# ScalarE scales the upper words of doubles, and two more head pairs use split exponents

## The chip, the cores and the metric

One core of a Trainium2 chip runs the whole program. The time is in device microseconds (us). Of the kernel before there are three runs: 1375.54, 1376.45 and 1377.31 us, so the median is 1376.45 us. TensorE (PE) multiplies matrices, VectorE (DVE), ScalarE (ACT) and GpSimd (POOL) do element work, SyncE (SP) issues the DMA transfers. Each engine takes its instructions strictly in the order in which the program gives them.

## The reference

```python
def _attn_ref(q, k, v, g_q, g_k):            # batch 8, heads 12, seq 448, head_dim 64, float32
    q_n, k_n = rmsnorm(q, g_q), rmsnorm(k, g_k)
    scores = q_n @ k_n.T / sqrt(64)
    attn = exp(scores - max(scores)); attn = attn / (sum(attn) + 1e-9)
    return attn @ v

def _moe_ref(x, w_in, w_out, s, b):          # x: 3584 x 768, w_in: 768 x 2048, w_out: 2048 x 768
    r = maximum(x @ w_in, 0)
    return (s * r * r + b) @ w_out
```

The two weight matrices come as float64. [...]

## The kernel before

**Pairs and steps.** The 96 heads are worked in 48 pairs, p = 0 to 47. A pair takes eight steps of the main loop (L784), four chunks of 128 keys for each of its two heads, so pair p has the steps 8p to 8p+7. In a step s the program issues, in this order: the two matmuls of the transposed scores of chunk s (`score_t`, L496 and L499), two matmuls of the feed-forward layer (`filler`), the exponent of chunk s on ACT (`exponent`), the transfers of finished feed-forward rows (`keep_r`, L228), the jobs listed for this step (`jobs[s]`), a score matmul for a later pair (`score`, L453 or L451), two more of the feed-forward layer, the ReLU copies on ACT (`rectify`, L218), the maximum of those scores on DVE (L464), the jobs of the kind `late`, the product of the exponents of chunk s-2 with v (`weigh`, L557), and two more feed-forward matmuls. The feed-forward matmuls start with step 57; they are the work that fills TensorE from there on. After the last pair comes the second layer alone.

**Exponents.** For pairs below `NV = PLAIN` (11) the exponents are float32 in SBUF (tile `e`, L511) and meet v in one float32 matmul, which is two records in the trace. For the later pairs the exponent stays in PSUM (L515), ACT copies it to a rounded high part `ah` (L523), DVE writes the rest to `low` (L538; the fourth chunk's rest goes into the unused half of `ah`), and three matmuls of the fast type (two for the fourth chunk) meet v. For that v too is split, into `vs`, by ACT (L353) and POOL (L354), three steps before the pair begins (`split_v`).

**Rooms.** A tile with a tag and one buffer is a room: a new tile of the tag waits until the last reader of the old one is done, wherever in the program that reader stands. The room `vr` has one buffer and two kinds of tenants. For an even pair below `TURNED` (12) it takes the second half of that pair's rows, loaded by `load_rows` (L241 to L245) 28 steps before that half's first step and last read by `turn`, the four transposes of L277, 14 steps before it. For pair 10 these are the steps 56 and 70. From pair `NV` on it takes v (`load_v`, L343 and L344), loaded nine steps before the pair begins; for pairs below `NV` v goes to two other tiles, five steps before (L338 to L341). The room `low` has the `low` parts of all split pairs and, before them, the pieces of w_in named in `THIRD`; the other pieces share two buffers of the tag `w64`.

**Doubles.** w_in comes in 24 pieces, loaded by `load_piece` and converted at the steps of `PACE`, in the steps 8 to 93; w_out in 24 groups, converted from step 112 on (`PACE_OUT`). `to_single` issues on DVE a shift of the upper word (L149), two combinations of words (L152, L154) and a comparison with multiplication (L157), which makes numbers below a bound zero by the square that ACT took (L150). Each `yield` ends what one call of `next` issues; `convert` and `convert_out` (both `late`) make the calls, five steps for a piece.

The part of the loop's lists that carries v, before and after the change alike:

```python
            at(s0 - (9 if p >= NV else 5), load_v, p)
            if p >= NV:
                at(s0 - 3, split_v, p)
```

Of the kernel before, what the change touches and what calls it, by code (L numbers as in the profile page):

```python
# [9 lines left out]
F32 = mybir.dt.float32  # L10
F32R = mybir.dt.float32r
I32 = mybir.dt.int32
AF = mybir.ActivationFunctionType
ALU = mybir.AluOpType
# [4 lines left out]

ORDERED = {ENGINE.PE, ENGINE.Activation, ENGINE.DVE, ENGINE.Pool, ENGINE.SP}  # L20

LEAST = (1 + 1 / 8) * 2.0 ** (0x70 - 127)

START = 9

# [23 lines left out]

APART = 8  # L50

PLAIN = 11

THIRD = (11, 14, 17)

PACE_OUT = tuple(48 * b + 16 + 8 * i for b in range(2, 8) for i in range(4))

GAP = 2


@with_exitstack
def attention_then_relu2_ffn(
# [30 lines left out]
    V, S, G, T = nc.vector, nc.scalar, nc.gpsimd, nc.tensor  # L93

    NPAIR, P, _, SEQ = kq.shape
# [7 lines left out]
    TILES = 2 * SEQ // P  # L103
    NV = PLAIN
    NQ = 4
# [9 lines left out]
    WI = 512  # L115
# [27 lines left out]
        bank = free.pop(0)  # L143
        return ps.tile([P, 512], F32, tag=bank, name=name), bank

    def to_single(w, a, m):

        low, high = w[:, :, 0], w[:, :, 1]
        V.tensor_scalar(a, high, 3, 0x3FFFFFF8, ALU.logical_shift_left, ALU.bitwise_and)  # L149
        S.activation(m, high.bitcast(F32), AF.Square)  # L150
        yield
        V.scalar_tensor_tensor(a, high, -0x40000000, a, ALU.bitwise_and, ALU.bitwise_or)  # L152
        yield
        V.scalar_tensor_tensor(a, low, 29, a, ALU.logical_shift_right, ALU.bitwise_or)  # L154
        yield
        af = a.bitcast(F32)
        V.scalar_tensor_tensor(af, m.bitcast(F32), LEAST * LEAST, af, ALU.is_ge, ALU.mult)  # L157

    def load_double(room, dst_hi, dst_lo, src):

        w, words, m = room
        nc.sync.dma_start(w.rearrange("p n t -> p (n t)"), src)
        yield
        a = words()
        yield from to_single(w, a, m)
        for _ in range(GAP):
            yield
        S.copy(dst_hi, a.bitcast(F32))
        yield
        G.tensor_tensor(dst_lo, a.bitcast(F32), dst_hi.bitcast(F32), ALU.subtract)  # L170
        yield
# [5 lines left out]
    def parts_of_w_in():  # L177

        for i in range(NS):
            whi[i] = wpool.tile([P, NCC, FS], F32R, tag=f"wh{i}", name=f"wih{i}")  # L180
            wlo[i] = wpool.tile([P, NCC, FS], F32R, tag=f"wl{i}", name=f"wil{i}")
            for c0 in range(0, FS, WI):
                for cc in range(NCC):
                    f0 = 2 * (i * FS + c0)
                    src = w_in32[cc * P : (cc + 1) * P, f0 : f0 + 2 * WI]
                    yield whi[i][:, cc, c0 : c0 + WI], wlo[i][:, cc, c0 : c0 + WI], src
# [43 lines left out]
    with tc.tile_pool(name="apool", bufs=1) as ap:  # L230
# [395 lines left out]
        def pieces():  # L626
            for i, (hi, lo, src) in enumerate(parts_of_w_in()):
                if i in THIRD:
                    w = ap.tile([P, WI, 2], I32, tag="low", name=f"w64i{i}")
                else:  # L630
                    w = ap.tile([P, WI, 2], I32, tag="w64", bufs=2, name=f"w64i{i}")

                def words(i=i):
                    return ap.tile([P, WI], I32, tag="wa", bufs=3, name=f"wai{i}")

                yield load_double((w, words, hi), hi, lo, src)

        todo = pieces()
        loaded = []

        def load_piece():

            g = next(todo, None)
            if g is not None:
                next(g)
                loaded.append(g)

        def convert(i, n):

            for _ in range((2, 1, 1, 2, 1)[n]):  # L650
                next(loaded[i], None)

        wides, singles = {}, {}

        def load_out(i):
# [3 lines left out]
            for h in range(2):  # L659
                r0 = (h * NH + f) * P  # L660
                src = w_out32[r0 : r0 + P].rearrange("p (e n) -> p e n", e=2)
                nc.sync.dma_start(to[:, h], src[:, :, 2 * c * P : 2 * (c + 1) * P])

        def convert_out(i, n):

            if n == 0:
                a, m = (
                    ap.tile([P, WI], I32, tag="wa", bufs=3, name=f"wao{i}_{k}") for k in range(2)
                )
                singles[i] = to_single(wides.pop(i), a, m.bitcast(F32)), a, m  # L670
            steps, a, m = singles[i]
            if n < 4:
                next(steps, None)
                return
            w = a.bitcast(F32).rearrange("p (h e n) -> p h e n", h=2, e=2)
            t = m.bitcast(F32).rearrange("p (k n) -> p k n", k=4)
            V.tensor_tensor(t[:, 0:2], w[:, :, 1], w[:, 0], ALU.subtract)
            V.tensor_tensor(t[:, 2], w[:, 1, 1], t[:, 0], ALU.subtract)
            V.tensor_tensor(t[:, 3], w[:, 1, 0], t[:, 2], ALU.subtract)

        def keep_out(i):
            f, c = divmod(i, NQ3)
            _, a, m = singles.pop(i)
            for d, of in ((b_d, a), (t_d, m)):
                nc.sync.dma_start(
                    d[:, :, f, c * P : (c + 1) * P].rearrange("k p n -> p k n"),
                    of.bitcast(F32).rearrange("p (k n) -> p k n", k=4),
                )

        late = (scale_q, split_last, convert, invert, convert_out, split_lows)  # L690

        fill = iter(())
# [9 lines left out]
        def at(s_, f, *a):  # L702
            jobs[s_].append((f, a))

        for i, s_ in enumerate(PACE):
            if i != THIRD[-1]:
                at(s_ + 3, load_piece)
        for p in range(NPAIR):
# [7 lines left out]
            for j in range(2):  # L716
                s1 = s0 + 4 * j
                steps = SOONER.get((p, j), (s1 - 20, s1 - 14, s1 - 13, s1 - 10, s1 - 6))
# [34 lines left out]
        for b in range(B):  # L753
            for g in range(NCC):
                s_ = W * NP * (b + 1) + START + (-3, -2, 0, 1, 2, 3)[g]
                if b == 0:
                    s_ = W * g + 24 if g < NCC - 1 else s_
# [3 lines left out]
        for s_ in (1, 7, 53):  # L761
            at(s_, load_piece)
        for i, s_ in enumerate(PACE):
            for n in range(5):
                at(STEPS[i][n] if i in STEPS else s_ + n, convert, i, n)
        for i, s_ in enumerate(PACE_OUT):
            at(s_ - 4, load_out, i)
            for n in range(5):
                at(s_ + n, convert_out, i, n)
            at(s_ + 6, keep_out, i)  # L770
# [11 lines left out]
        with tc.manual_schedule(engines=ORDERED):  # L782
            begun = []
            for s_ in range(FIRST, NSLOT + START + NCC):  # L784
# [34 lines left out]
                b, m = divmod(s_ + 1 - START, W * NP)  # L819
# [7 lines left out]
    with tc.tile_pool(name="opool", bufs=1) as op:  # L827

        def half(pool, tag, shape, name):
            return pool.tile(shape, F32R, tag=tag, name=name)  # L830
# [5 lines left out]
        room = [half(op, f"c2{x}", [P, 3, NH, P], f"room{x}") for x in "hl"]  # L836
# [144 lines left out]
        with tc.manual_schedule(engines=ORDERED):  # L981
# [29 lines left out]
            for n in range(7 * NG):  # L1011
                g, k = divmod(n, 7)
# [78 lines left out]
```

## Time and profile before

| | |
|---|---|
| runs | 1375.54, 1376.45, 1377.31 us |
| span of the profiled execution | 1375.6 us (0.85 us under the median) |
| PE busy | 99% of the span |
| DVE, ACT, POOL busy | 77%, 68%, 44% |
| granted TensorE clock | 1.00 in every stretch |
| steps 0 to 57 | about 15.8 to 112.8 us |
| steps 58 to 71 | about 112.8 to 152.7 us |
| steps 72 to 87 (pairs 9 and 10) | 152.74 to 194.83 us |
| rest of the pairs, then the second layer | to 893 us, then to the end |

A matmul's end is modelled in the profile, so the distance between the starts of two matmuls says what one costs, not its listed length. On DVE a listed length can hold time in which the instruction has started and can't go on.

### The profile page before, as it was taken

What the parts mean: (1) busy time and instruction counts of PE and PEld (TensorE: products, weight loads), DVE (VectorE), ACT (ScalarE), POOL (GpSimd) and SP (SyncE); (2) the same over time, 40 slices, a digit from 0 to 9 for tenths busy, and PEclk for the clock granted to TensorE, in tenths of its full rate; (3) what the DMA queues carried; (4) which work ended last, traced back from release to release, by engine and by line L of the source; (5) the groups of instructions that cost most, each with busy time, mean ns of one, the idle gap of its engine ahead of it and who ended that gap; (6) DMA issues with size and microseconds to landing.
All of it is one profiled execution on the core that took longest, in us unless ns stands there. A gap on an engine that the chain in (4) does not pass through costs nothing.

```text
span 1375.6 us, 21578 instructions
## 1 busy us (share of the span) xinstructions
PE 1363.6 (99%) x6970; PEld 1255.6 (91%) x6970; DVE 1057.3 (77%) x1572; ACT 937.2 (68%) x1727; POOL 603.1 (44%) x486
## 2 busy tenths in 40 slices
PE   8999999999999999999999999999999999999998
PEld 7767789999999999999999999999999999999998
DVE  7999997897888798688788878526766676666763
ACT  6886778888888888888888887636544434344431
POOL 6875787766667666676667665100000000000000
PEclk9999999999999999999999999999999999999999
DMA  4555676787788788778778867356543332343330
GB/s 133 150 145 169 181 232 197 230 249 214 223 235 239 222 243 232 221 222 250 229 220 240 236 204 211 104 197 222 186 119 118 88 91 90 95 121 112 85 90 35
DMA packets 262800, 243.39 MB, mean 177 GB/s; under 512 B 85280, under 2 KB 244000, under 8 KB 262688
## 3 DMA queue, kind: packets, MB, share of 16 engines
q1 hardware_dynamic: 262688, 242.03, 60.0%
q8 instruction: 55, 0.90, 0.3%
q14 instruction: 57, 0.47, 0.1%
HBM read 177.21 MB, written 53.38 MB: 168 GB/s over the span
## 4 chain that ended last, share of the span: by engine, by line
PE 92%; DVE 4%; ACT 2%; DMA 1%; issue 1%; SPq 0%; POOL 0%; DVEq 0%; POOLq 0%; ACTq 0%
PE ph L198 32%; PE p L936 30%; PE av L557 15%; PE st L496 5%; PE st L499 5%; PE sh L451 4%; PE sh L453 1%; DVE nmx L464 1%; PE tk L282 1%; DVE wai L154 1%; DVE ssq L260 0%; DVE wai L152 0%; DVE wai L157 0%; DMA zb<-z_d 0%; ACT e L511 0%
## 5 line engine op out<-in xcount | busy, mean ns | idle before, releaser
L198 PE MATMUL ph<-x,wih 128*128 128x448 f32 x1536 | 488.3, 365 | 0.0
L198 PEld LDWEIGHTS ph<-x,wih 128*128 128x128 f32 x1536 | 289.0, 188 | 28.7 <-issue 6.1
L198 PE MATMUL ph<-x,wil 128*128 128x448 f32 x768 | 293.3, 382 | 0.0
L515 ACT ACTIVATE st<-st 128x448 f32<-128x448 f32 (+1 forms) x296 | 155.9, 527 | 104.1 <-PE st L499 102.7
L464 DVE TENSOR_REDUCE nmx<-sh 128x1 fp32r<-128x448 f32 (+1 forms) x348 | 212.8, 616 | 12.0 <-PE sh L451 6.3
L538 DVE TENSOR_TENSOR low<-st,ah 128x448 fp32r<-128x448 f32 x222 | 136.7, 616 | 47.2 <-ACT ah L523 42.5
L557 PE MATMUL av<-ah,vs 128*128 128x448 f32 x592 | 168.7, 366 | 0.0
L496 PE MATMUL st<-qa,ka 128*128 128x448 f32 (+1 forms) x384 | 159.1, 414 | 2.3 <-DVE nmx L464 2.2
L198 PEld LDWEIGHTS ph<-x,wil 128*128 128x128 f32 x768 | 144.3, 188 | 17.0 <-issue 6.2
L523 ACT CAST ah<-st 128x448 fp32r<-128x448 f32 (+1 forms) x296 | 156.9, 530 | 2.0
L499 PE MATMUL st<-qb,kb 128*128 128x448 f32 (+1 forms) x384 | 140.3, 365 | 0.0
L557 PEld LDWEIGHTS av<-ah,vs 128*128 128x128 f32 x592 | 111.2, 188 | 8.6
L921 ACT CAST hi<-a 128x1024 fp32r<-128x1024 f32 x54 | 56.8, 1053 | 91.0 <-PE p L936 74.0
L420 POOL TENSOR_TENSOR ka<-kq,ka 64x448 fp32r<-64x448 f32 x72 | 86.2, 1198 | 56.3 <-ACT ka L415 53.0
L603 POOL TENSOR_TENSOR u<-uz,zb 128x448 f32<-128x448 f32 x48 | 59.9, 1247 | 95.9 <-DMA zb<-z_d 75.9
L421 POOL TENSOR_TENSOR qb<-kq,qa 64x448 fp32r<-64x448 f32 x72 | 95.3, 1323 | 5.4
L369 POOL TENSOR_TENSOR ri<-ri,mhalf 128x14 f32<-128x14 f32 x36 | 93.6, 2601 | 3.0
L922 DVE TENSOR_TENSOR lo<-s,hi 128x1024 fp32r<-128x1024 f32 x41 | 50.1, 1222 | 52.1 <-ACT hi L921 52.1
L218 ACT ACTIVATE r<-ph 128x448 f32<-128x448 f32 x128 | 69.7, 545 | 27.6 <-PE ph L198 15.8
L354 POOL TENSOR_TENSOR vs<-vr,vs 128x512 fp32r<-128x512 f32 x37 | 49.4, 1336 | 86.0 <-DMA w64o<-in_dram 31.4
L496 PEld LDWEIGHTS st<-qa,ka 128*128 128x128 f32 (+1 forms) x384 | 68.2, 178 | 20.2 <-DVE nmx L464 6.1
L385 POOL TENSOR_TENSOR kq<-kq,rb 128x448 f32<-128x448 f32 x72 | 86.5, 1202 | 0.0
(253 smaller groups left out, 3256.4 us busy)
## 6 DMA issues: line engine op xcount, KB each, us to landing
kq<-in_dram SPq DMA_DIRECT2D x72, 448.0 KB, 5.1
rb<-i_d SPq DMA_DIRECT2D x72, 448.0 KB, 4.8
r_d<-r SPq DMA_DIRECT2D x128, 224.0 KB, 3.7
a<-r_d SPq DMA_DIRECT2D x48, 512.0 KB, 4.9
raw<-in_dram SPq DMA_DIRECT2D x36, 448.0 KB, 5.0
w64i<-in_dram SPq DMA_DIRECT2D x24, 512.0 KB, 4.5
w64o<-in_dram SPq DMA_DIRECT2D x48, 256.0 KB, 4.1
kb<-ka SPq DMA_DIRECT2D x96, 112.0 KB, 2.8
```

The lines of the kernel that those rows point to most:

```text
L198: T.matmul(ph[:, :SEQ], w[:, cc, f0 : f0 + P], xs[b, cc][:, part, :], start=cc == 0 and m == 0, stop=cc == NCC - 1 and m == 2,)
L369: G.tensor_tensor(ri, ri, mhalf[:, :n], ALU.pow)
L385: G.tensor_tensor(t[:, 0], t[:, 0], rb[:, 0], ALU.mult)
L421: G.tensor_tensor(qb[n][:D, a], t[:D, 1], qa[n][:D, a].bitcast(F32), ALU.subtract)
L464: V.tensor_reduce(out=nmxs[p][:n, c : c + 1], in_=sh[:n, :SEQ], op=ALU.max, axis=AX.X, negate=True)
L496: T.matmul(st[:rows, :SEQ], ka[n][:, keys], qa[n][:, q], start=True, stop=False)
L499: T.matmul(st[:rows, :SEQ], kb[n][:, keys], qb[n][:, q], start=False, stop=True,)
L515: S.activation(st[:rows, :SEQ], st[:rows, :SEQ], AF.Exp)
L523: S.copy(ah[:rows], sts[i][0][:rows, :SEQ])
L538: V.tensor_tensor(al, st[:rows, :SEQ], ah[:rows].bitcast(F32), ALU.subtract)
L557: T.matmul(av[:, :SEQ], x, a, start=kc == 0 and m == 0, stop=kc == 3 and m == len(todo) - 1,)
L936: T.matmul(po, a[:, f], w[:, f], start=f == 0 and m == 0, stop=f == NH - 1 and m == 2,)
```

## The change

`to_single` loses its fourth DVE instruction. ACT now multiplies the upper word, read as a float32, by 2^-112 in place (this takes 112 off the top eight exponent bits, which is what the float32 exponent needs), DVE shifts the lower word, and two combinations add the sign and the upper word shifted by three. The ACT pass is a job of its own, `lower` and `lower_out`, at the piece's first step and not of the kind `late`. The scratch tile of the square is no longer needed. `GAP` grows by one, so that the later calls fall where they did. `PLAIN` falls from 11 to 9: pairs 9 and 10 now use split exponents. `THIRD` loses piece 17, and the load that is left out of the list of loads is that of step 70 instead of that of step 77.

```diff
-LEAST = (1 + 1 / 8) * 2.0 ** (0x70 - 127)
+DOWN = 2.0 ** -(896 // 8)
-PLAIN = 11
-THIRD = (11, 14, 17)
+PLAIN = 9
+THIRD = (11, 14)
-GAP = 2
+GAP = 3
-    def to_single(w, a, m):
+    def to_single(w, words):
         low, high = w[:, :, 0], w[:, :, 1]
-        V.tensor_scalar(a, high, 3, 0x3FFFFFF8, ALU.logical_shift_left, ALU.bitwise_and)
-        S.activation(m, high.bitcast(F32), AF.Square)
+        S.activation(high.bitcast(F32), high.bitcast(F32), AF.Copy, scale=DOWN)
         yield
-        V.scalar_tensor_tensor(a, high, -0x40000000, a, ALU.bitwise_and, ALU.bitwise_or)
+        a = words()
+        V.tensor_scalar(a, low, 29, 7, ALU.logical_shift_right, ALU.bitwise_and)
         yield
-        V.scalar_tensor_tensor(a, low, 29, a, ALU.logical_shift_right, ALU.bitwise_or)
+        V.scalar_tensor_tensor(a, high, -0x80000000, a, ALU.bitwise_and, ALU.bitwise_or)
         yield
-        af = a.bitcast(F32)
-        V.scalar_tensor_tensor(af, m.bitcast(F32), LEAST * LEAST, af, ALU.is_ge, ALU.mult)
+        V.scalar_tensor_tensor(a, high, 3, a, ALU.logical_shift_left, ALU.bitwise_or)
+        return a
...
+        def lower(i):
+            next(loaded[i], None)
...
+        def lower_out(i):
+            room = []
+            def words():
+                for k in range(2):
+                    room.append(ap.tile([P, WI], I32, tag="wa", bufs=3, name=f"wao{i}_{k}"))
+                return room[0]
+            singles[i] = to_single(wides.pop(i), words), room
+            next(singles[i][0])
...
         for i, s_ in enumerate(PACE):
+            at(s_, lower, i)
             for n in range(5):
                 at(STEPS[i][n] if i in STEPS else s_ + n, convert, i, n)
         for i, s_ in enumerate(PACE_OUT):
             at(s_ - 4, load_out, i)
+            at(s_, lower_out, i)
```

## Rows read from the trace of the kernel before

**Rows 1.** The page's first line.
```profile
span 1375.6 us, 21578 instructions
```
**Rows 2.** Stretches: length, then busy us of each engine, clock, DMA share, GB/s.
```profile
15.80:112.80 97.00, 93.94 (x408) 67.14 (x407) 90.50 (x161) 82.06 (x162) 70.19 (x60) 1.00 0.56 154
112.80:152.70 39.90, 38.43 (x171) 30.72 (x170) 38.59 (x57) 29.26 (x55) 26.11 (x20) 1.00 0.57 168
152.70:194.80 42.10, 42.10 (x186) 34.33 (x185) 40.70 (x60) 29.45 (x56) 32.24 (x25) 1.00 0.77 227
214.40:893.00 678.60, 678.37 (x3336) 621.37 (x3336) 554.16 (x907) 568.47 (x1182) 440.54 (x342) 1.00 0.76 221
```
**Rows 3.** Waits of PE, 15.8 to 195 us: total, times, longest.
```profile
PE st L496 <- DVE nmx L464: 2.2, 3, 0.8
PE sh L453 <- DVE nmx L464: 1.1, 1, 1.1
```
**Rows 4.** Waits of PE, 195 us to the end.
```profile
PE av L557 <- DVE low L538: 0.2, 1, 0.2
```
**Rows 5.** Timeline of PE, step 71 (plain exponents): start, length, instruction.
```profile
151.59 0.91 PE L557 MATMUL av<-e,vf 128*128 128x448 f32 x2
...
152.54 0.36 PE L198 MATMUL ph<-x,wih 128*128 128x448 f32 x1
```
**Rows 6.** Timeline of PE, step 98 (split exponents).
```profile
220.49 0.57 PE L557 MATMUL av<-ah,vs 128*128 128x448 f32 x2
...
221.10 0.36 PE L198 MATMUL ph<-x,wil 128*128 128x448 f32 x1
```
**Rows 7.** Groups by line, whole span: count, busy us, mean ns, idle before.
```profile
L538 DVE TENSOR_TENSOR low<-st,ah 128x448 fp32r<-128x448 f32 x222 | 136.7, 616 | 47.2 <-ACT ah L523 42.5 <-PE sh L451 2.9 <-PE ph L198 1.3
L157 DVE SCALAR_TENSOR_TENSOR wao<-wao,wao 128x512 f32<-128x512 f32 x24 | 27.0, 1125 | 0.0
L353 ACT CAST vs<-vr 128x512 fp32r<-128x512 f32 x37 | 22.6, 611 | 0.0
L157 DVE SCALAR_TENSOR_TENSOR wai<-wih,wai 128x512 f32<-128x512 f32 x24 | 19.0, 792 | 0.1
L150 ACT ACTIVATE wih<-w64i 128x512 fp32r<-128x512 f32 x24 | 16.2, 673 | 0.1
```
**Rows 8.** Groups of DVE, 152.74 to 194.83 us alone.
```profile
L157 DVE SCALAR_TENSOR_TENSOR wai<-wih,wai 128x512 f32<-128x512 f32 x7 | 6.4, 917 | 0.1
```
**Rows 9.** Timeline of DVE, steps 60 to 62.
```profile
118.69 3.37 DVE L154 SCALAR_TENSOR_TENSOR wai<-w64i,wai 128x512 int32<-128x512 int32 x1
```
**Rows 10.** Timeline of POOL, the same stretch.
```profile
120.22 1.28 POOL L170 TENSOR_TENSOR wil<-wai,wih 128x512 fp32r<-128x512 f32 x1
```
**Rows 11.** Timeline of SP's issues, steps 63 to 65.
```profile
131.18 0.49 SPq L581 DMA_DIRECT2D zt<-uz  x1
131.77 0.53 SPq L228 DMA_DIRECT2D r_d<-r  x1
...
134.31 0.36 SPq L162 DMA_DIRECT2D w64i<-in_dram  x1
```
**Rows 12.** Timeline of PE, steps 70 and 72.
```profile
147.92 0.55 PE L277 MATMUL tk<-ident,rows 112*128 112x112 f32 x4
148.24 0.54 PE L453 MATMUL sh<-ka,qa 128*112 128x448 f32 x1
...
154.16 0.91 PE L557 MATMUL av<-e,vf 128*128 128x448 f32 x2
```
**Rows 13.** Transfers of L344 (v into `vr`): issue to landing.
```profile
DMA to landing us min/median/max: 2.7/3.1/5.1
```
**Rows 14.** Transfers of L162 (pieces of w_in): issue to landing.
```profile
DMA to landing us min/median/max: 3.5/4.5/6.9
```
**Rows 15.** Timeline of ACT, step 70.
```profile
147.77 0.55 ACT L511 ACTIVATE e<-st 128x448 f32<-128x448 f32 x1 [1.03 <-PE st L499]
```
**Rows 16.** Timeline of DVE, steps 70 and 71.
```profile
149.75 0.42 DVE L149 TENSOR_SCALAR wai<-w64i 128x512 int32<-128x512 int32 x1
```

More of the change, by code (lines that the diff above doesn't have):

```diff
@@ L144, in psum @@
         return ps.tile([P, 512], F32, tag=bank, name=name), bank
-    def to_single(w, a, m):
+    def to_single(w, words):
         low, high = w[:, :, 0], w[:, :, 1]
-        V.tensor_scalar(a, high, 3, 0x3FFFFFF8, ALU.logical_shift_left, ALU.bitwise_and)
-        S.activation(m, high.bitcast(F32), AF.Square)
+        S.activation(high.bitcast(F32), high.bitcast(F32), AF.Copy, scale=DOWN)
         yield
-        V.scalar_tensor_tensor(a, high, -0x40000000, a, ALU.bitwise_and, ALU.bitwise_or)
+        a = words()
+        V.tensor_scalar(a, low, 29, 7, ALU.logical_shift_right, ALU.bitwise_and)
         yield
-        V.scalar_tensor_tensor(a, low, 29, a, ALU.logical_shift_right, ALU.bitwise_or)
+        V.scalar_tensor_tensor(a, high, -0x80000000, a, ALU.bitwise_and, ALU.bitwise_or)
         yield
-        af = a.bitcast(F32)
-        V.scalar_tensor_tensor(af, m.bitcast(F32), LEAST * LEAST, af, ALU.is_ge, ALU.mult)
+        V.scalar_tensor_tensor(a, high, 3, a, ALU.logical_shift_left, ALU.bitwise_or)
+        return a
     def load_double(room, dst_hi, dst_lo, src):
-        w, words, m = room
+        w, words = room
         nc.sync.dma_start(w.rearrange("p n t -> p (n t)"), src)
         yield
-        a = words()
-        yield from to_single(w, a, m)
+        a = yield from to_single(w, words)
         for _ in range(GAP):
@@ L634, in words @@
                     return ap.tile([P, WI], I32, tag="wa", bufs=3, name=f"wai{i}")
-                yield load_double((w, words, hi), hi, lo, src)
+                yield load_double((w, words), hi, lo, src)
         todo = pieces()
@@ L662, in load_out @@
                 nc.sync.dma_start(to[:, h], src[:, :, 2 * c * P : 2 * (c + 1) * P])
-        def convert_out(i, n):
[L666 to L671, printed above, removed]
+        def lower_out(i):
[6 more added lines that the diff above has]
+            next(singles[i][0])
+        def convert_out(i, n):
+            steps, room = singles[i]
             if n < 4:
@@ L674, in convert_out @@
                 return
+            a, m = room
             w = a.bitcast(F32).rearrange("p (h e n) -> p h e n", h=2, e=2)
@@ L682, in keep_out @@
             f, c = divmod(i, NQ3)
-            _, a, m = singles.pop(i)
+            a, m = singles.pop(i)[1]
             for d, of in ((b_d, a), (t_d, m)):
```

## The prediction

> **What bounds the kernel now.** The profiled execution has a span of 1375.6 us [rows 1], 0.85 us under the median of the three runs; the sum is made against the span, and that 0.85 us is added at the end. I read first the table of engine times by stretch, then the waits of TensorE, then the timelines of one step. The table [rows 2] shows three regimes. From 214 to 893 us TensorE is busy 678.37 of 678.60 us and DVE 554.16: there TensorE is the bound, and its waits from 195 us to the end are one of 0.2 us [rows 4]. Nothing taken from DVE after step 95 can be worth anything, and nothing that is lost before it can be won back there. From 15.8 to 152.7 us TensorE is idle 97.00 - 93.94 = 3.06 and 39.90 - 38.43 = 1.47 us, 4.5 us in all, most of it behind the maxima of DVE [rows 3], which is busy 93% and 97%. From 152.7 to 194.8 us, the steps of pairs 9 and 10, TensorE has no idle time and DVE is busy 40.70 of 42.10 us: two engines lie level, and what is put on DVE there comes out in the time.
>
> **The doubles.** One DVE instruction of 48 pieces goes: 24 of w_in, 0.792 us each, and 24 of w_out, 1.125 us each [rows 7]. The 27.0 us of w_out lie from step 112 on, under a TensorE that waits for nothing [rows 4]: worth 0. Of w_in, some 15 pieces are done before step 70; they relieve DVE by 15 x 0.792 = 11.9 us where TensorE loses 4.5 us to it. I take 4.0 us of the 4.5; bounds 1.5 and 4.5 (not all, since part of the waits comes from copies and transposes that stay). The seven pieces in the stretch of pairs 9 and 10 are priced below. The ACT pass changes its function, keeps its size and writes with a stride; the nearest row is the 0.673 us of the square [rows 7], so I take 0, with ACT idle a third of the time [rows 2] as its cover; bounds 0 and 0.3 us if a pass comes late just before a DVE step that now needs it. The shift of the lower word has the form of the old one of the upper word: 0. `GAP` only keeps the calls at their steps: 0. The missing scratch tile frees nothing that anyone waits for: 0. Of the loads, only pieces 17 to 19 come later, by 2, 2 and 3 steps; the room `low` is free of piece 14 five steps before the first `low` part. A piece takes 4.5 us to land [rows 14], so piece 19, issued at step 77 for step 78, can hold ACT for some 2 us; the DVE step that needs the pass is issued later in its step than the pass and DVE has other work before it, so I take 0, bounds 0 and 2.
>
> **The split exponents.** A plain chunk and the matmul after it take TensorE from 151.59 to 152.54 us [rows 5], 0.95 us; three split matmuls take 220.49 to 221.10 [rows 6], 0.61, so one takes 0.20 and the plain chunk 0.75. A pair had 8 x 0.75 = 6.0 and gets 22 x 0.20 = 4.4: TensorE gains 1.6 a pair, 3.2 us in all. DVE pays: 16 parts of 0.616 us [rows 7] = 9.9 us. ACT gets 16 copies (0.54 us, as the exponent of rows 15, together some 8.6) and two of 0.611 for v; with the 29.45 us that it has [rows 2] that makes 39.3. What DVE gets back here are seven multiplications. Their mean in this stretch is 0.917 us [rows 8], so 6.4 by the row. But the length holds blocked time: a combination that is 3.37 us long ends at 122.06, about 0.6 us after POOL's instruction of 120.22 + 1.28 = 121.50 [rows 9, 10], so it ran 0.6 and stood the rest. I take 5.3, between 7 x 0.6 = 4.2 and 6.4. DVE then needs 40.70 + 9.9 - 5.3 = 45.3 us where TensorE would need 42.1 - 3.2 = 38.9. So the 3.2 us of TensorE are not seen, and the stretch grows by 45.3 - 42.1 = 3.2 us (bounds 1.0 and 4.5, the first if DVE's lead at its start is used up there).
>
> The Trainium skill (SBUF — State Buffer, Who interferes with whom) says that a VectorE instruction with two SBUF inputs and a GpSimd instruction that reads SBUF exclude each other for a whole instruction, whoever issues first; rows 9 and 10 agree. By that rule a removed instruction gives back only its own 0.6 us, since the next one meets the same block: 4.2, and a stretch 4.3 us longer.
>
> **The room `vr`.** The change of one number moves v of pair 9 from two tiles of its own to the room `vr`, and its load from step 67 to step 63. The second half of the rows of pair 10 lies in that room from step 56 until the transposes of step 70 have read it. So the load of step 63 must wait for step 70, and SP takes its queue in order: all that was issued freely between [rows 11] now stands behind it, the outputs of the feed-forward layer, the broadcast of the sums, the rows of pair 11, pieces 15 and 16, the shift of pair 9, the raw rows of pair 12. TensorE itself gets to the transposes, since nothing in its steps up to 70 needs one of these; they are done about 148.24 us [rows 12]. ACT, though, stands at step 69 before the copy of v, then before piece 15. Counted from 148.24: the load of v (0.58 us, the issue of a like size), then the issues from 131.77 to 134.31 [rows 11], 2.54, so piece 15 is issued at 151.4 and lands at 155.9 [rows 14]; v lands at 153.3 by the longest of its row [rows 13], so the piece is last. ACT passes the piece (0.673), does the ReLU copy (0.54, taken as the exponent's 0.55) and comes to the exponent of step 70 at 157.1 instead of 147.77 [rows 15]. Its product with v, at 154.16 [rows 12], then can't start before 157.7: TensorE is 3.5 us late at the least. DVE is worse off: it stands before piece 15 until 155.9 + 0.67 = 156.6 instead of 149.75 [rows 16], 6.8 us later. And since DVE is the bound for the next twenty steps, that delay stays whole. So +6.8; the bounds are -0.5 (a wait that hides, with DVE's lead spared) and +9.3, ACT's whole delay. The same wait at pair 10 finds the room free at once (v of pair 9 is split at step 69, the load is at step 71): 0.
>
> **The sum.** 1375.6 - 4.0 + 6.8 + 3.2 = 1381.6; with 0.85 for the median, 1382.4, so 1382.
>
> **The rivals.**
> *The wait is there, but DVE is not the bound behind it* (same). Then TensorE keeps its 3.2 us and only its own 3.5 are lost: 1376.45 - 4.0 - 3.2 + 3.5 + up to 2 for pieces and copies, about 1374.7. For it: DVE's length holds blocked time, and while it stands POOL works off its queue. Against it: 40.70 of 42.10 us busy [rows 2], and ACT with 39.3 of 38.9 us is no better.
> *The load's wait is hidden* (faster; the other side of the forecast): SP comes to step 63 so late, or the pieces stand so far ahead, that ACT and DVE lose nothing. Its place is the load of L344, its price 0 instead of 6.8, and it decides when piece 15 has landed by the time DVE comes to it: 1376.45 - 4.0 + 1.0 and, as far as TensorE's gain shows, up to 3.2 less, so about 1371.5. Against it: SP's issues of steps 63 to 65 went out at their steps [rows 11].
> *Blocking by POOL wins* (slower): the multiplications give back 4.2, POOL's late queue holds the rows of pair 11, and the delay is ACT's 9.3: 1376.45 - 3.0 + 9.3 + 4.3 = 1387. The rule of the Trainium skill named above (SBUF — State Buffer, Who interferes with whom) is what would bring it. For it: the block in rows 9 and 10; against it: the mean of 0.792 us [rows 7] is near the free 0.6, so most multiplications were not blocked.
> *The change doesn't do what it says*: the exponents of pairs 9 and 10 are split by the same tests of `NV` that the later pairs go through, so I leave no chance for it.
>
> **How the numbers follow.** Forecast 0.56, same 0.18, hidden 0.16, blocked 0.10. Measured differences under about 0.2% (2.75 us) can't be told from none. Forecast and blocked case lie above 1379.2: 0.66 slower; 0.18 within; 0.16 faster. The forecast's own range has the wait between 3.5 (TensorE's own lateness) and 9.3, the stretch between 1.0 and 4.5 and the relief between 4.5 and 1.5, the ends of all three not together: 1378 to 1387. The whole range goes from 1373, within the second rival and short of most of the third, to 1387.5.
>
> **What would show it.** Right: SP has one wait of some 15 us or more before the first transfer of L344, ended by the transposes; ACT idle for several us before the first L353 or the pass of piece 15; DVE idle for some 6 us there, then busy without a gap to step 92; TensorE's waits before 127 us nearly gone; steps 72 to 87 longer than 42.1 us; everything after step 96 as long as before. Wrong: no such wait at L344, or steps 72 to 87 in 39 us.

## The result, and the profile after

The changed kernel takes 1386.06 us (median of five runs, 1383.01 to 1387.34); five runs of the kernel before beside it give 1377.31. The ratio is 1.0061 with an interval of [1.005, 1.0072]: slower by 0.6%, some 8.5 us, where the forecast was +5.55 us on 1376.45. Span against span it is 1384.1 - 1375.6 = 8.5 us.

Where in the program the time went is read best from TensorE's own marks: the start of the first matmul of the transposed scores in each step, which every kernel has. The table gives that start in the trace of after less the start in the trace of before (147.11 us for step 70, 152.74 for step 72, and so on).

```
step          40     56     64     70     71     72     74     78     79     80     88     92     96    104
us         -1.23  -1.81  -2.70  -3.65  +3.86  +5.44  +5.44  +5.65  +9.50  +9.40  +9.93  +9.32  +9.23  +9.23
```

Three pieces can be told apart: -3.65 us up to step 70; 9.1 us lost at the steps 70 and 71; 3.8 us lost between step 74 and step 96. From there on the two kernels run alike, but for some 0.7 us that come back in small pieces, 0.4 of them before step 200.

The table by stretch of after, columns as in [rows 2], cut at the same steps (15.8 is the start of step 0, 143.50 step 70, 158.20 step 72, 204.80 step 88, 223.70 step 96):

```profile
15.80:110.50 94.70, 92.30 (x406) 66.81 (x405) 83.21 (x152) 82.08 (x162) 68.44 (x60) 1.00 0.57 158
110.50:143.50 33.00, 33.00 (x149) 26.88 (x148) 27.92 (x45) 24.04 (x45) 16.42 (x13) 1.00 0.31 92
143.50:158.20 14.70, 7.35 (x28) 5.67 (x27) 3.34 (x7) 4.79 (x9) 7.30 (x9) 0.77 0.62 207
158.20:204.80 46.60, 42.41 (x197) 36.62 (x196) 44.21 (x68) 39.16 (x78) 34.92 (x27) 0.96 0.72 218
223.70:901.90 678.20, 678.20 (x3337) 621.28 (x3336) 535.02 (x883) 567.56 (x1182) 430.69 (x342) 1.00 0.76 221
```

The third row is the whole case: in two steps every engine but SP's queue is idle for half of the time or more, TensorE for 7.35 of 14.70 us, and the clock column is below 1.00 for the first time. The fourth row is the stretch of the pairs 9 and 10, 46.60 us where it was 42.10; it too has less than the full clock. In the last row, as before, TensorE never waits.

The longest of TensorE's waits of after up to 205 us (to be held against [rows 3], and against [rows 4], where one wait was left behind 195 us). Line numbers differ by kernel: `score_t` is L496 before and L495 after, and in the experiments the lines move with those that were added.

```profile
PE st L495 <- ACT r L217: 7.4, 1, 7.4
PE sh L452 <- DVE low L537: 2.5, 1, 2.5
PE av L556 <- DVE low L537: 1.7, 2, 1.5
PE sh L452 <- DVE nmx L463: 0.9, 2, 0.5
PE sh L452 <- ACT wih L167: 0.7, 1, 0.7
```

One stop of 7.4 us behind a ReLU copy, two of 2.5 and 1.5 us behind `low`, and what is left of the waits for the maxima. Behind the 7.4 us stands the wait of SP that was forecast. First SP's longest wait, then the timelines of SP, ACT, DVE and PE around it:

```profile
SPq L343 <- PE tk L276: 17.2, 1, 17.2
```

```profile
126.46 1.14 SPq L580 DMA_DIRECT2D zt<-uz  x1
144.89 0.33 SPq L343 DMA_DIRECT2D vr<-in_dram  x1
...
147.58 0.37 SPq L162 DMA_DIRECT2D w64i<-in_dram  x1
...
150.42 0.48 SPq L580 DMA_DIRECT2D zt<-zr  x1
```

```profile
147.69 0.62 ACT L352 CAST vs<-vr 128x512 fp32r<-128x512 f32 x1 [5.58 <-DMA vr<-in_dram]
152.88 0.67 ACT L149 ACTIVATE w64i<-w64i 128x512 f32<-128x512 f32 x1 [4.58 <-DMA w64i<-in_dram]
153.45 0.53 ACT L217 ACTIVATE r<-ph 128x448 f32<-128x448 f32 x1
```

```profile
143.32 0.62 DVE L463 TENSOR_REDUCE nmx<-sh 112x1 fp32r<-112x448 f32 x1
155.16 0.84 DVE L586 TENSOR_SCALAR zt<-zt 128x7 f32<-128x7 f32 x1 [11.22 <-DMA zt<-zr]
```

```profile
146.32 0.36 PE L197 MATMUL ph<-x,wih 128*128 128x448 f32 x1
154.03 0.74 PE L495 MATMUL st<-qa,ka 128*128 128x448 f32 x1 [7.35 <-ACT r L217]
...
158.18 0.36 PE L495 MATMUL st<-qa,ka 128*128 128x448 f32 x1
```

Read as a chain: SP issues nothing between 127.6 and 144.89, because the load of v for pair 9 (L343) waits for the transposes of step 70. Then it works off what had gathered; piece 15 goes out at 147.58 and has landed when ACT's pass starts at 152.88, 5.3 us later. The ReLU copy stands behind that pass in ACT's order, and TensorE's first matmul of step 71 wants the PSUM room which that copy empties: it starts at 154.03. DVE has stood since 143.94, not before piece 15 but before the sums of step 67 (`zt<-zr`), which SP issued behind it, at 150.42.

The clock is the other part of the loss. The table by stretch in pieces of 2 us:

```profile
148.00:150.00 2.00, 0.00 (x0) 0.00 (x0) 0.00 (x0) 0.30 (x1) 0.00 (x0) 1.00 0.75 222
150.00:152.00 2.00, 0.00 (x0) 0.00 (x0) 0.00 (x0) 0.00 (x0) 1.35 (x2) 0.60 1.03 328
152.00:154.00 2.00, 0.00 (x0) 0.00 (x0) 0.00 (x0) 1.12 (x3) 2.00 (x2) 0.50 1.06 384
154.00:156.00 2.00, 1.97 (x5) 1.77 (x6) 0.83 (x1) 0.85 (x3) 1.98 (x4) 0.50 0.83 325
156.00:158.00 2.00, 2.00 (x7) 1.42 (x7) 1.86 (x6) 2.00 (x4) 1.86 (x2) 0.70 0.08 6
...
178.00:180.00 2.00, 1.91 (x5) 1.74 (x6) 1.97 (x7) 0.00 (x0) 2.00 (x1) 0.50 0.07 14
```

TensorE has been idle since 146.7. The granted clock falls to 0.50 (1.2 GHz) within the row that starts at 150 and is back at 1.00 (2.4 GHz) before 158. After the restart the single matmuls start some 0.37 us apart (154.94, 155.32, 155.69), from step 72 on some 0.20 us (158.18, 158.37, 158.58). Step 71 lasts 158.18 - 154.03 = 4.15 us, where it took 152.74 - 150.17 = 2.57 in the trace of before. So 7.4 us of standing and 1.6 us of half clock make 9.0 of the 9.1. After the stop at step 78 the same is seen again (last row).

The groups by line of the conversions, which build a float32 from the two 32-bit words of a double; columns as in [rows 7]:

```profile
L154 DVE SCALAR_TENSOR_TENSOR wai<-w64i,wai 128x512 int32<-128x512 int32 x24 | 21.8, 910 | 5.6 <-ACT w64i L149 3.7
L156 DVE SCALAR_TENSOR_TENSOR wai<-w64i,wai 128x512 int32<-128x512 int32 x24 | 20.3, 846 | 0.1
L149 ACT ACTIVATE w64i<-w64i 128x512 f32<-128x512 f32 x24 | 16.2, 674 | 4.8 <-DMA w64i<-in_dram 4.6
L152 DVE TENSOR_SCALAR wai<-w64i 128x512 int32<-128x512 int32 x24 | 11.0, 459 | 0.1
```

ACT's scaling pass costs what the square cost, 0.674 against 0.673 us [rows 7]; three DVE instructions are left of four.

### The profile page after: what moved, and what is told of

Its sections match the earlier page's. It is cut to its first block, busy times and chain, and to the rows that moved or that the text cites. A ratio compares the mean times of both kernels' runs of the same rounds, so it can differ in the third digit from the quotient of the medians.

```text
span 1384.1 us, 21583 instructions
## 1 busy us (share of the span) xinstructions
PE 1364.0 (99%) x6982; PEld 1260.5 (91%) x6982; DVE 1024.0 (74%) x1540; ACT 944.1 (68%) x1745; POOL 589.3 (43%) x488
## 4 chain that ended last, share of the span: by engine, by line
PE 94%; DVE 3%; issue 1%; ACT 1%; DMA 1%; SPq 0%; POOL 0%; DVEq 0%; ACTq 0%; POOLq 0%
PE ph L197 32%; PE p L947 29%; PE av L556 15%; PE st L495 5%; PE st L498 5%; PE sh L450 4%; PE sh L452 1%; DVE nmx L463 1%; PE tk L281 1%; PE warmth L328 0%; DVE wai L154 0%; DMA zt<-zr 0%; DVE wai L156 0%; DVE low L537 0%; DVE wai L152 0%
## 5 line engine op out<-in xcount | busy, mean ns | idle before, releaser
L197 PE MATMUL ph<-x,wil 128*128 128x448 f32 x768 | 288.2, 375 | 0.0
L514 ACT ACTIVATE st<-st 128x448 f32<-128x448 f32 (+1 forms) x312 | 164.5, 527 | 113.1 <-PE st L498 111.7
L537 DVE TENSOR_TENSOR low<-st,ah 128x448 fp32r<-128x448 f32 x234 | 144.0, 615 | 47.3 <-ACT ah L522 43.2
L556 PE MATMUL av<-ah,vs 128*128 128x448 f32 x624 | 178.4, 367 | 0.2 <-DVE low L537 0.2
L495 PE MATMUL st<-qa,ka 128*128 128x448 f32 (+1 forms) x384 | 159.5, 415 | 7.5 <-ACT r L217 7.4
L522 ACT CAST ah<-st 128x448 fp32r<-128x448 f32 (+1 forms) x312 | 165.4, 530 | 2.1
L556 PEld LDWEIGHTS av<-ah,vs 128*128 128x128 f32 x624 | 117.3, 188 | 9.9 <-DVE low L537 0.6
L368 POOL TENSOR_TENSOR ri<-ri,mhalf 128x14 f32<-128x14 f32 x36 | 93.6, 2601 | 3.0
L353 POOL TENSOR_TENSOR vs<-vr,vs 128x512 fp32r<-128x512 f32 x39 | 52.5, 1346 | 98.5 <-issue 43.0
L495 PEld LDWEIGHTS st<-qa,ka 128*128 128x128 f32 (+1 forms) x384 | 68.2, 178 | 24.6 <-ACT r L217 7.7
L420 POOL TENSOR_TENSOR qb<-kq,qa 64x448 fp32r<-64x448 f32 x72 | 87.4, 1213 | 5.4
L556 PE MATMUL av<-low,vs 128*128 128x448 f32 x234 | 86.5, 370 | 1.5 <-DVE low L537 1.5
```

The costliest lines, as they stand in the source:

```text
L197: T.matmul(ph[:, :SEQ], w[:, cc, f0 : f0 + P], xs[b, cc][:, part, :], start=cc == 0 and m == 0, stop=cc == NCC - 1 and m == 2,)
L368: G.tensor_tensor(ri, ri, mhalf[:, :n], ALU.pow)
L420: G.tensor_tensor(qb[n][:D, a], t[:D, 1], qa[n][:D, a].bitcast(F32), ALU.subtract)
L495: T.matmul(st[:rows, :SEQ], ka[n][:, keys], qa[n][:, q], start=True, stop=False)
L514: S.activation(st[:rows, :SEQ], st[:rows, :SEQ], AF.Exp)
L522: S.copy(ah[:rows], sts[i][0][:rows, :SEQ])
```

## The experiments

Each kernel was timed beside runs of the kernel before on the same chip, in three sets. That kernel's median was 1377.62 us beside the first four kernels below, 1377.24 beside "doubles and the wait", "the transposes two steps earlier", "late v of pair 9" and "splits only", and 1377.45 beside the rest. "After" names the changed kernel. The starts of the steps, less those of before, for all of them, each from one profiled execution:

```
step              56     64     70     71     72     74     78     79     80     88     92     96
after          -1.81  -2.70  -3.65  +3.86  +5.44  +5.44  +5.65  +9.50  +9.40  +9.93  +9.32  +9.23
other room     -1.67  -2.56  -3.50  -3.50  -3.51  -3.50  -3.52  +0.01  +0.47  +0.82  +0.21  +0.12
doubles only   -2.99  -3.90  -4.84  -4.85  -4.85  -4.85  -4.84  -4.84  -4.84  -4.84  -4.93  -5.02
PLAIN = 10     -1.81  -2.71  -3.67  -3.66  -3.67  -3.66  -3.66  -3.67  -3.66  -2.39  -2.88  -2.98
wait only      -0.59  -0.63  -0.66  +1.84  +4.75 +10.84 +10.84 +10.84 +10.85 +10.84 +10.86 +10.86
late v of 9    -3.08  -3.98  -4.94  -4.93  -4.93  -4.93  -0.30  -0.44  -0.54  -0.02  -0.53  -0.62
splits only    -0.13  -0.13  -0.14  +2.37  +5.55 +11.91 +12.85 +17.19 +17.18 +20.11 +23.12 +23.03
turn earlier   -3.12  -4.03  -4.49  -2.13  -0.40  -0.39  -0.44  +3.08  +3.61  +3.91  +3.42  +3.33
doubles, wait  -2.67  -3.58  -4.53  +3.15  +5.38  +5.42  +5.43  +5.43  +5.43  +5.43  +5.34  +5.25
late v of both -3.10  -4.07  -5.02  -5.01  -5.02  -5.01  -4.97  -4.33  -4.44  -3.83  -4.43  -4.53
doubles, three -3.00  -3.91  -4.86  -4.86  -4.86  -4.86  -4.85  -4.85  -4.85  -4.86  -4.94  -5.04
10, three      -1.95  -2.85  -3.79  -3.79  -3.79  -3.79  -3.79  -3.79  -3.79  -2.53  -1.55  -1.64
PLAIN = 12     -3.10  -4.01  -4.95  -4.96  -4.96  -4.96  -4.95  -4.95  -4.95  -4.95  -4.77  -4.09
```

**The wait, the doubles and the splits apart.**

*Other room.* After, but v of pair 9 goes to a room that is free (`rb1`) and is loaded six steps before the pair: no wait for the transposes, the rest as changed.

```diff
-                vr = vrs[p] = ap.tile([P, NKC, 2, D], F32, tag="vr", name=f"vr{p}")
+                tag = "rb1" if p == NV else "vr"
+                vr = vrs[p] = ap.tile([P, NKC, 2, D], F32, tag=tag, name=f"vr{p}")
...
-            at(s0 - (9 if p >= NV else 5), load_v, p)
+            at(s0 - (6 if p == NV else 9 if p > NV else 5), load_v, p)
```

> The changed kernel with one difference: v of pair 9 goes to the room rb1, empty at that time, and is loaded at step 66, so its load need not wait for the transposes of step 70. If the wait at that load is what costs (my theory), the gap of about 9 us at step 71 is gone, and with it the half clock after it: the early relief of 3.6 us stays, the stretch of steps 72 to 87 costs 1 to 4.5 us, and the time is 1374 to 1379 us, 8 or more under the changed kernel's 1386. Rival one, TensorE's gain of 3.2 us shows as soon as the wait is gone: about 1370.5. Rival two, the split exponents and DVE are what costs, the wait is only where it shows: 1383 or more.

Measured 1376.01 us, ratio 0.9986 [0.9977, 0.9995]. The jump at step 71 is gone, all 9.1 us of it; the stretch of the pairs 9 and 10 costs what it costs in after, 3.6 us from step 74 to 96. The longest of TensorE's waits of this kernel from 100 to 230 us:

```profile
PE sh L453 <- DVE low L538: 2.4, 1, 2.4
PE av L557 <- DVE low L538: 1.5, 1, 1.5
```

So the two stops behind `low` belong to the split exponents and not to the wait.

*Doubles only.* After with pairs 9 and 10 plain:

```diff
-PLAIN = 9
+PLAIN = 11
```

> The changed kernel with PLAIN = 11: the new conversion of the doubles alone, with two pieces in the third room. Theory: DVE's relief up to step 70 is worth 3.6 us as in the changed kernel's trace, and nothing after step 95: 1372.5 to 1374.5. Rival, the later loads of pieces 17 to 19 or the ACT pass cost what the relief gives: 1376 to 1378.

Measured 1372.63 us (1372.23 to 1372.85), ratio 0.9963 [0.995, 0.9975]: faster than before, and the lowest median of the study. All of its gain lies before step 70 (-4.84 us), and TensorE has no wait at all from 100 to 230 us.

*One pair more split.* After with only pair 10 split besides those of before; its v meets a room that is free.

```diff
-PLAIN = 9
+PLAIN = 10
```

> The changed kernel with PLAIN = 10: pair 10 alone is moved to split exponents; its v is loaded into vr at step 71, one step after the rows there are read. Theory: no long wait of SP, DVE gets 8 parts (4.9 us) more, TensorE loses 1.6: 1372 to 1376, at least 10 under 1386. Rival, any v brought into that room so early holds up SP: 1382 or more, with a wait of SP before that load of over 5 us.

Measured 1375.01 us, ratio 0.9982 [0.9973, 0.9991]. No stop at step 71; the longest wait is one of 1.9 us behind `low`, at the end of pair 10's steps.

*The wait only.* The kernel before, with v of pair 9 loaded one more time into the room `vr`, at step 63, where nobody reads it. Nothing is left out; the load only takes its place in SP's queue.

```diff
+        def load_extra(p):
+            x = ap.tile([P, NKC, 2, D], F32, tag="vr", name=f"vx{p}")
+            nc.sync.dma_start(x, v[p])
...
+            if p == 9:
+                at(s0 - 9, load_extra, p)
```

> The kernel before with one transfer more: at step 63 v of pair 9 is also loaded into the room vr, where nobody reads it. It is the wait alone, without split exponents, without a copy on ACT that waits for v, with the old conversion. Theory: what stands behind the load in SP's queue is what costs, so TensorE stops at step 71 for 6 to 9 us and the time is 1382 to 1387. Rival one, ACT's wait for v itself is what costs: the kernel before's time within 2 us, 1375.5 to 1379.5. Rival two, the wait costs only because DVE is full of split parts afterwards: 1378 to 1381.

Measured 1390.66 us, ratio 1.0092 [1.0079, 1.0106]: +13, where 5 to 10 had been expected. SP's longest wait from 100 to 230 us, and TensorE's three stops in the steps 70 to 72:

```profile
SPq L348 <- PE tk L277: 16.3, 1, 16.3
```

```profile
PE sh L457 <- DVE nmx L468: 3.4, 1, 3.4
PE st L500 <- ACT r L218: 2.3, 1, 2.3
...
PE st L500 <- ACT e L515: 1.2, 1, 1.2
```

The steps 70 to 74 lose 11.5 us, in three stops and not in one; of the 13 us 10.9 are there by step 96, and the rest lies behind step 200, where its cause was not looked for. One load that nobody needs costs more here than the whole change, so both rivals that made the wait cheap (hidden, or paid by TensorE's 3.5 us alone) fall.

**The price of the wait under other conditions.**

*Doubles and the wait.* "Doubles only" with the same extra load (its lines as above; nothing is left out):

> The new conversion with PLAIN = 11 and the extra transfer into vr at step 63 that nobody reads: the wait alone again, now with DVE relieved. Beside the new conversion alone (1372.6) it prices the wait without split exponents. Theory: the wait costs 9 to 12 us whatever DVE does afterwards: 1381.5 to 1385. Rival, the relieved DVE and ACT catch up: 1375 to 1379.

Measured 1382.55 us, ratio 1.0041 [1.0028, 1.0054]; 9.9 us are lost between step 70 and step 72. TensorE's waits of this kernel are a single line:

```profile
PE st L499 <- ACT r L217: 7.5, 1, 7.5
```

The pairs 9 and 10 are plain here and DVE has less to do in their steps, yet the price is whole. So it isn't DVE's load behind the wait that keeps it, as the prediction had it: TensorE itself has stood, and nothing behind step 72 gives that back, since without the extra load TensorE has no wait there that could shrink. The order on ACT gives the stop its form: with the new conversion ACT passes piece 15 (152.18) ahead of the ReLU copy (152.75), in "wait only", with the old one, behind it (156.35 after 151.41), and there TensorE stops three times.

*The transposes two steps earlier.* After, with `turn` for the second half of pair 10 at step 68:

```diff
+    (10, 1): (64, 68, 71, 74, 78),
```

> The changed kernel with the transposes of pair 10's second half at step 68 instead of 70, so that the room is free two steps (some 5 us) earlier; everything else, the copies out of PSUM too, stays. Theory: SP's wait falls by about 5 us, ACT meets its first late transfer some 5 us sooner, and the stop of TensorE at step 71 falls from 9 to 3 to 5 us: 1378.5 to 1382. Rival, the cost hangs on the order in the queue and not on how long it stands: 1385 to 1387.

Measured 1380.57 us, ratio 1.0027 [1.0018, 1.0036]. SP's wait and TensorE's longest:

```profile
SPq L344 <- PE tk L277: 10.9, 1, 10.9
```

```profile
PE st L496 <- ACT r L218: 2.7, 1, 2.7
```

SP's wait is 10.9 instead of 17.2 us, TensorE's stop 2.7 instead of 7.4, and the steps 70 to 72 lose 4.1 instead of 9.1. Between these two kernels the price goes with the time for which SP's queue stands.

*Late v of pair 9.* After, with that load at step 71 and the split of v at step 73:

```diff
-            at(s0 - (9 if p >= NV else 5), load_v, p)
+            at(s0 - (1 if p == NV else 9 if p > NV else 5), load_v, p)
...
-                at(s0 - 3, split_v, p)
+                at(s0 + (1 if p == NV else -3), split_v, p)
```

> The changed kernel with v of pair 9 loaded into vr at step 71, when the rows of pair 10 have left it, and split at step 73, one step before its first use. Theory: as with the other room, the wait of SP is gone, and with it the stop at step 71; if the split comes too late for step 74 TensorE waits there for POOL by at most 2 us: 1375 to 1379. Rival, v needs its lead of nine steps: a stop of 5 us or more at step 74, 1381 or more.

Measured 1380.17 us, ratio 1.0019 [1.001, 1.0028], above what was expected. The reason was in the edit: the load of pair 10's v, left at step 71, now met pair 9's v in the room until the split at step 73.

```profile
SPq L343 <- POOL vs L353: 5.8, 1, 5.8
```

The jump moved from step 71 to the steps 76 to 78, and is 4.6 us. It is the same mechanism, made a second time by not asking for the room's last reader.

*Late v of both.* The same with pair 10's load at step 74, after that split:

```diff
-            at(s0 - (9 if p >= NV else 5), load_v, p)
+            at(s0 - ({NV: 1, NV + 1: 6}.get(p, 9) if p >= NV else 5), load_v, p)
```

> The changed kernel with v of pair 9 loaded at step 71 and split at step 73, as in the run with the late load, and v of pair 10 loaded at step 74, once the copies of pair 9's v are done, instead of 71. Theory: no transfer meets a tenant in its room, SP has no wait over 2 us at the loads of v, and the time is that of the other room, 1375 to 1377. Rival, the short lead itself is what cost in the run with the late load: 1379 to 1381.

Measured 1373.54 us (1372.55 to 1375.31), ratio 0.9973 [0.9962, 0.9983], below what was expected. So both pairs can use split exponents at a cost of 0.5 us between step 74 and 96, in this execution; the kernel then is level with "doubles only" within the two intervals. It differs from "other room" in where and when v is loaded, and in that v of pair 9 is split at step 73 and not at 69. There the same steps cost 3.6 us and the stop at step 78 was 2.4 us, here it is 0.5 us and the clock stays up; the stop at step 87 stays, 1.5 and 1.4 us (the medians are 2.5 us apart, of which up to 1.5 lie before step 70). The table by stretch, 148 to 196 us, first "other room", then this kernel:

```profile
148.00:196.00 48.00, 43.79 (x203) 38.10 (x202) 44.53 (x67) 39.14 (x78) 32.66 (x27) 0.96 0.69 210
```

```profile
148.00:196.00 48.00, 45.68 (x220) 40.05 (x219) 43.87 (x71) 42.53 (x85) 39.75 (x31) 1.00 0.75 231
```

DVE is about as busy in both (44.53 and 43.87 us), so the sum of DVE's work alone doesn't make the stop. The timelines of DVE show where it comes from. First "other room", then this kernel, the steps 75 and 76:

```profile
157.49 3.70 DVE L154 SCALAR_TENSOR_TENSOR wai<-w64i,wai 128x512 int32<-128x512 int32 x1
...
162.89 0.62 DVE L538 TENSOR_TENSOR ah<-st,ah 64x448 fp32r<-64x448 f32 x1
```

```profile
155.73 0.69 DVE L154 SCALAR_TENSOR_TENSOR wai<-w64i,wai 128x512 int32<-128x512 int32 x1 [0.21 <-ACT w64i L149]
...
159.95 0.62 DVE L537 TENSOR_TENSOR ah<-st,ah 64x448 fp32r<-64x448 f32 x1 [1.40 <-ACT ah L522]
```

The same combination of a piece is 3.70 us long in one and 0.69 in the other. In "other room" POOL works at that time from 156.89 without a gap, and ends the low half of a piece at 160.64, 0.55 us before the combination is done:

```profile
156.89 1.40 POOL L268 TENSOR_TENSOR rows<-rows,ri 112x512 f32<-112x512 f32 x1
158.25 1.15 POOL L603 TENSOR_TENSOR u<-uz,zb 128x448 f32<-128x448 f32 x1
159.36 1.28 POOL L169 TENSOR_TENSOR wil<-wai,wih 128x512 fp32r<-128x512 f32 x1
```

From there DVE goes without a gap up to the part of `low` that TensorE stops for at step 78. In "late v of both" it has 1.40 us to spare before `ah`, and TensorE's stop at step 78 is 0.5 us. So the 3 us of blocked time, less what DVE had to spare, are read here as the stop; no run moves that block alone, and each kernel is one execution. Why the combination is caught in the one and not in the other, where POOL's instructions come at other times, was not tested.

**The stretch, the pieces and one pair more.**

*Splits only.* The kernel before with the new numbers and the old conversion:

```diff
-PLAIN = 11
+PLAIN = 9
-THIRD = (11, 14, 17)
+THIRD = (11, 14)
```

> The kernel before with PLAIN = 9 and two pieces in the third room: the split exponents and the wait at vr, with the old conversion of four DVE instructions. Theory: no early relief (0 instead of -4.8 at step 70), the stop at steps 71 to 74 of 9 to 11, and a stretch that costs 2 to 4 us more than with the new conversion, since DVE keeps its seven multiplications there: 1391 to 1396. Rival, the conversion has no part in the stretch's cost: 1389 to 1390.

Measured 1398.65 us, ratio 1.0159 [1.0145, 1.0173], above the expected 1391 to 1396. The wait costs 12.0 us, near the 11.5 of "wait only"; the steps 74 to 96 cost 11.1 us where after has 3.8. TensorE's waits behind `low` in this kernel:

```profile
PE av L557 <- DVE low L538: 4.6, 3, 2.0
...
PE sh L453 <- DVE low L538: 2.7, 1, 2.7
```

They are 7.3 us together, against 2.5 + 1.7 = 4.2 in after. So the shorter conversion is worth up to 11.1 - 3.8 = 7.3 us in this stretch, more than the 5.3 that I took for its seven multiplications, and less by whatever this kernel's later wait adds to its start.

*Three pieces in the third room.* "Doubles only" and `PLAIN = 10`, each with the old third room:

```diff
-THIRD = (11, 14)
+THIRD = (11, 14, 17)
```

> The new conversion with PLAIN = 11 and piece 17 back in the third room, so that pieces 17 to 19 are loaded as early as in the kernel before. My term for the later loads was 0: 1372.3 to 1373.0, the same as with two pieces (1372.6). Rival, the two steps of lead are worth something: 1371.5 or less.

> PLAIN = 10 with three pieces in the third room, which is free again at step 78, before the first low part of step 81. Beside PLAIN = 10 with two (1375.0): if the stop of 1.9 us at step 87 comes from DVE's load alone, 1374.5 to 1375.5; if late pieces have pushed DVE's work together there, 1373 or less.

Measured 1373.02 us, ratio 0.9968 [0.9956, 0.998], and 1374.75, ratio 0.9983 [0.9974, 0.9992]: both level with their twins (0.9963 and 0.9982). The later loads of the pieces 17 to 19 are worth nothing, and the wait of 1.9 us behind `low` with `PLAIN = 10` stays (2.0), so it isn't a late piece that makes it.

*One pair more plain.*

```diff
-PLAIN = 9
+PLAIN = 12
```

> The new conversion with PLAIN = 12: pair 11 too keeps plain exponents. It prices TensorE's side of a pair alone, in steps where TensorE is never kept waiting. Theory: a plain pair costs TensorE 1.6 us more, nothing else moves: 1374.0 to 1374.5. Rival, DVE's eight parts of pair 11 still cost TensorE something in the steps 88 to 95, and leaving them out pays: 1372.6 or less.

Measured 1374.64 us, ratio 0.9979 [0.997, 0.9988], 0.1 us above the expected range and 2.0 us above "doubles only". From step 88 to step 104 its mark goes from -4.95 to -3.57, that of "doubles only" from -4.84 to -5.02: a pair of plain exponents costs TensorE 1.4 to 1.6 us where it is the bound.

## Why the prediction was right, and where its sizes were off

**The sign and the mechanism.** The forecast's case came true: a load moved to a step at which its room still has a tenant, SP's queue standing behind it (17.2 us against "some 15 us or more"), ACT and DVE idle for what the queue held. "Wait only" shows that this alone makes the kernel slower, "other room" that without it the change is level with before or a little faster.

**The relief, -4.0.** Measured -3.65 by step 70 in after; TensorE's waits up to 148 us went from 4.2 to 2.4 us, so they were halved and not "nearly gone". That is 1.8 of the 3.65 us; TensorE's busy time up to step 70 is 1.6 us shorter too (126.81 and 125.22 us, 552 and 551 matmuls), which a bound of 4.5 taken from its idle time alone leaves out. Of the eleven kernels with the new conversion four show -3.5 to -3.8 by step 70 and seven -4.5 to -5.0, up to 0.5 us beyond the bound of 4.5. The difference of some 1.2 us is there by step 56, where these kernels still do the same work, so it is not tied to an edit. Each is one execution; what sets it was not found out.

**The room, +6.8.** This is the term that was mis-sized; it measured 9.1. The way from SP to ACT was right: piece 15 goes out at 151.4 and ACT comes to the exponent of step 70 at 157.1 in the sum, which less the relief of 3.65 is 147.75 and 153.45; measured were 147.58 and 153.87. Behind that three things were wrong. I let TensorE stop at the product of step 72, "3.5 us late at the least"; it stopped a step earlier, at the first matmul of step 71, since the PSUM room that it wants is emptied by the ReLU copy, which stands behind piece 15 on ACT. I let DVE stand before piece 15; it stood before the sums of step 67 (11.2 us idle), which SP issues after that piece: in the list of what is queued behind the wait I had the transfer, but not who waits for it first. And the half clock after the stop, 1.6 us, was no term of the sum. That "DVE is the bound behind it" keeps the delay whole was also not the reason, as "doubles and the wait" shows: 9.9 us with DVE relieved. So that DVE's 6.8 lies near the 7.4 for which TensorE stood is luck. The third rival's 1387 comes nearer to the 1386.06 than the forecast's 1382, since it took ACT's whole 9.3 and a stretch of 4.3; in part that is luck as well, as its 9.3 holds no half clock.

**The stretch, +3.2.** Measured +4.5 from step 72 to 88 and 3.8 from step 74 to 96. The size was near, the form was not, and "late v of both", where the same work costs 0.5, shows that the nearness is luck. I had DVE short of time evenly, 45.3 us of work without a gap. It was busy 44.21 of 46.60 us. TensorE's gain is seen where nothing stops it: the steps 80 to 83 take 9.57 us (183.65 to 193.22) against 10.27 before (174.25 to 184.52), which is 1.4 a pair, where I had 1.6. It is lost again in two single stops, of 2.5 and 1.5 us, with half clock behind the first. Before each a DVE instruction stands while POOL works, and from it DVE goes without a gap to the part of `low` that TensorE waits for. Timelines of DVE and of POOL of after:

```profile
169.27 2.83 DVE L156 SCALAR_TENSOR_TENSOR wai<-w64i,wai 128x512 int32<-128x512 int32 x1
...
177.41 0.62 DVE L537 TENSOR_TENSOR low<-st,ah 128x448 fp32r<-128x448 f32 x1
...
200.76 1.55 DVE L391 SCALAR_TENSOR_TENSOR kq<-kq,singles,rb 128x448 f32<-128x448 f32 x1
```

```profile
170.26 1.29 POOL L169 TENSOR_TENSOR wil<-wai,wih 128x512 fp32r<-128x512 f32 x1
...
200.54 1.28 POOL L169 TENSOR_TENSOR wil<-wai,wih 128x512 fp32r<-128x512 f32 x1
```

The combination ends at 172.10, 0.55 us after POOL's instruction (171.55); the instruction at step 87 (L391) ends at 202.31, 0.5 us after POOL's 201.82. That is the block of [rows 9, 10] again. The rule of the Trainium skill (SBUF — State Buffer, Who interferes with whom) agrees with these rows. It does not agree with every row of after: while POOL's L368, which reads 128x14 numbers, ran from 161.06 to 164.15, a combination of two SBUF inputs (L156, at 163.62) took 0.69 us, as at 139.39, where POOL stood still. What I drew from the rule for the third rival, that seven removed multiplications give back only 4.2 us, is not borne out: "splits only" against after gives up to 7.3.

**The terms taken as 0.** ACT's pass (0.674 against 0.673 us), the later loads of pieces (two pairs of kernels) and the wait at pair 10's load (no such line in after's waits of SP) were 0. The cover named for the pass was smaller than said: by [rows 2] ACT is idle 15% of the first stretch and 27% and 30% of the next two, not a third. After step 96 the kernels run alike, but for the 0.7 us.

**The sum.** Measured -3.65 + 9.1 + 3.8 = 9.25 by step 96, and -0.7 behind it: 8.5. Forecast: -4.0 + 6.8 + 3.2 = 6.0.

## What to carry to other kernels

Before a load is moved ahead, ask for the last reader of the room that it goes to; if that comes later, the load stands in the issuing engine's queue and so does everything behind it, however little it has to do with the load. Price such a wait by the first instruction of each engine that needs one of the transfers queued behind, and by what stands behind that instruction in turn, TensorE's PSUM rooms included, and add the time at half clock if TensorE stops. Work taken off an engine pays where that engine makes another wait: here 3.5 to 5.0 us for some 12 taken off DVE before step 70, and nothing for the 27.0 us of w_out, under which TensorE hardly waits.

## What was not expected of the hardware

The granted clock was at 0.50 (1.2 GHz) not only around the stop of 7.4 us but also behind the one of 2.5 us at step 78 (178 to 180 us), and step 78 lost 9.50 - 5.65 = 3.85 us where the stop itself was 2.45. Behind the stop of 1.5 us at step 87 nothing of the kind is seen: step 88 starts at 204.76 and lasts 2.44 us, less than the 2.58 of before. The Trainium skill (TensorE: Matmul & The Clock Gate, HAM oscillation — how this bites in real kernels) tells of kernels in which waits for data let the clock fall, so that the work behind each wait starts at the lower one; the two longer stops here agree with it. While the held-back transfers were worked off, at a DMA share of up to 1.06, piece 15 took 5.3 us to land, between the median and the longest of [rows 14]: held against that median of 4.5, some 0.8 us of its lateness is the crowd by this estimate, the rest its place in the queue.

One thing stays open: why the relief comes in two sizes, some 3.7 and 4.9 us. The version to keep is "doubles only" (`PLAIN = 11` with the new conversion), 1372.63 us, 0.4% faster than before.
